# Small matmuls of the delta rule between two feed-forward layers: four groups a chunk instead of six

## The chip, the cores and the metric

The kernel runs on one core of one Trainium2 chip. The metric is the device time in microseconds (us), the median of the runs shown. Lower is better.

## The reference

A delta rule over 768 tokens (4 batches, 8 heads, 48 features a head) feeds two feed-forward layers of 3072 tokens, 384 features and 2048 hidden units:

```python
for t in range(S):
    kt, vt, bt = (k_n[:, :, t], v[:, :, t], beta[:, :, t, None])
    y[:, :, t] = np.einsum('bhd,bhde->bhe', q[:, :, t], state)
    v_old = np.einsum('bhde,bhd->bhe', state, kt)
    state = state + bt[:, :, :, None] * np.einsum('bhd,bhe->bhde', kt, vt - v_old)
# y becomes x: 3072 tokens x 384
h = x @ w_in                      # layer 1
g = np.where(pos, h, np.where(neg, 0.0, (h + beta) ** 2 / (4.0 * beta)))
x = g @ w_out
h = x @ w_in2; r = np.maximum(h, 0.0); out = (r * r) @ w_out2     # layer 2
```

## The kernel before

**The delta rule** goes by 24 chunks of 32 tokens (128 rows: 4 batches x 32 tokens). For each chunk, `chunk_steps` (L391) returns six steps, each a run of 64 small matmuls on TensorE, one for each pair of (head, batch), except the last:

- `ks` (L411): K S, keys times the state, into a bank of PSUM with the tag `att`; VectorE subtracts it from the value (L416).
- `tr` (L418): W R, the inverted triangle times that residual, into another `att` bank; ScalarE copies it to U (L428).
- `qs` (L430): Q S, into an `att` bank that stays in use until `pu` is done. Behind it the keys of the chunk after the next five are loaded on SP (`load_kq(c + 6)`).
- `ku` (L446): K' U, added to the state in its own PSUM banks; VectorE and ScalarE copy the state to SBUF (L456, L457). The last chunk has none.
- `pu` (L437): P U, added to Q S in its bank; ScalarE copies the sum to Y (L444).
- `xt` (L467): three 128x128 transposes of Y, from which ScalarE and VectorE make the input of layer 1 (L476, L477).

The matmuls of `ks` and `qs` have a 48x32 stationary operand, those of `tr` and `pu` one of 32x32, those of `ku` one of 32x48. There are two `att` banks.

**The gram** of a chunk (L260) gives K K' and Q K' by 64 more small matmuls (48x32 stationary) into an `att` bank, which VectorE masks (L284) into `gp`. When four chunks of a group have theirs, `tri` (L314) inverts their triangles: VectorE transposes `gp` (L325), a short run of VectorE, ScalarE and GpSimd instructions scales it, GpSimd does 29 dependent steps of two instructions each (L370, L376), and VectorE transposes the result back (L380). The next group's `tr` needs that.

**Layer 1** goes by nine blocks of 2 or 3 chunks (SIZES) and 16 hidden units of 128 in each. `hidden` makes a unit's nine 128x128 matmuls into the one bank `h` (two sums of hi parts and lo parts: six with `xh`, three with `xl`), ScalarE and VectorE the activation; `out1` takes nine more two units later into the `acc` banks. Layer 2 does the same with eight blocks and no chunk steps beside it.

**The order on TensorE is written out by hand** (`manual_schedule` with PE alone, L660); the order on the other engines is the scheduler's. Each hidden unit of a block has two slots: one right behind `hidden` (L773) and one right behind `out1` (L778), so that a block has 32. The loop at L703 to L719 lists the steps and grams that belong to a block's time (those of the next block's chunks) and spreads them: entry i of n goes to slot i * 32 // n (in the first block over 24 slots, from the ninth on). In a full block that is 18 steps and 3 to 5 grams. `ready` and `at` remember the slots of a gram and of a chunk's first step; `tri` is called one slot after the last gram of its group, its end is called at the slot of the first step that needs it (L733 to L735).

Of the kernel before, what the change touches and what calls it, by code (L numbers as in the profile page):

```python
# [17 lines left out]

# Chunks of the blocks in which the first layer takes them
SIZES = [2, 2, 3, 3, 3, 3, 3, 2, 3]  # L20
# and of the groups whose triangles are inverted together
GROUPS = [4] * 6
# [3 lines left out]
def kernel(  # L26
# [8 lines left out]
):  # L35
    """The delta rule in chunks of T tokens, with keys as they come (K, not normalised):
    with n = |k| + 1e-6 and g = beta / n**2,
        W = inverse(1 + diag(g) strictlower(K K')) diag(g),  U = W (diag(n) V - K S),
        Y = Q S + strictlower(Q K') U,                       S <- S + K' U.
    Its result goes through the two feed-forward layers, whose float32 products are sums of  # L40
    products of exact parts: x = hi + lo, 12 bits each (float32r).

    kq:   [chunk, (batch % 2, feature), (batch // 2, head, key tokens | query tokens)]
    kv:   [chunk, (batch, token), (key | value, head, feature)]
    beta: [(batch, chunk of the group, head), group, token]
    w1, w2: [128 hidden, in | out, partition, column], the bits of float64
    out:  [chunk, (batch, token), feature]
    """
    nc = tc.nc
# [10 lines left out]
    GFIRST = [sum(GROUPS[:g]) for g in range(NG)]  # L60
    GC = T // H               # chunks of a full group
    NM = NCH // NC            # blocks of the second layer
    N = NC * P
    LAG = 2
    LENT = 28                 # weights whose bits may lie in the last weights' place
    RG = 3
    RAW = 3
    WT, WL = 3, 4
    GB = 2
    MANY = 4                  # first hidden units that may use the chunks' banks  # L70
    HEAD = 8                  # slots of the first block without steps of the second's chunks

# [16 lines left out]
    def weight(i, f):  # L89
        """(hi, lo) of hidden units f's weights: in (i = 0), out (1)."""  # L90
        if (i, f) not in pairs:
            t = wp.tile([P, 2, DM], F32R, tag=f"w{i}{f}", name=f"w{i}{f}")
            pairs[i, f] = t[:, 0], t[:, 1]
        return pairs[i, f]

    s_ps = [ps.tile([P, H, D], F32, name=f"sps{i}") for i in range(B2)]

    # Until the first layer begins, its banks serve the chunks too.
    early = ["att", "acc0", "att", "acc1", "acc2"]
# [15 lines left out]

# [1 line left out]
    def load_kq(c, tag="kqt", bufs=6):  # L117
# [13 lines left out]

    # A weight comes as the bits of a float64: words (low, high).  The high word, read as a
    # float32 and scaled by 2**-112, has its exponent rebiased; shifted left by 3 it is the
    # weight's leading 21 bits as a float32.  The low word adds the last 3 bits, rounded to
    # nearest, but never up into the leading ones.
    raws = {}

    # The last weights' place takes some of the first ones' bits.
    def load_w(x, key):
# [6 lines left out]

    # The second layer's weights become float32.
    def convert_stages(key, box):
# [20 lines left out]

    # The first layer's become their two parts, x = hi + lo.  # L170
    def part_stages(key, box):
# [13 lines left out]
    def weight_items(w):  # L185
        # A hidden unit's second weights are needed LAG units after its first.
        keys = [(w, f, i) for f in range(NF) for i in range(2)]
        if w == 0:
            keys.sort(key=lambda k: (k[1] + LAG * k[2], -k[2]))

        def item(x):
            _, f, i = keys[x]
            box = {}
            if w == 0:
                r = part_stages(keys[x], box)
            else:
                r = convert_stages(keys[x], box)
                r.append(lambda: nc.sync.dma_start(w2f[f, :, i], box["t"]))
            s1 = r[1]
            r[1] = lambda: (s1(), ahead(x + 1))  # L200
            return r

        # Loads run ahead of the conversions by the buffers there are.
        todo = list(enumerate(keys))

        def ahead(x):
            end = x + RAW
            if w == 0 and end < LENT:
                end = min(end + 2, LENT)
            while todo and todo[0][0] < end:  # L210
                load_w(*todo.pop(0))

        return lambda: ahead(0), [item(x) for x in range(len(keys))]
# [18 lines left out]

# [1 line left out]
    def norm_stages(ss, sm):  # L234
        """n = sqrt(ss) + 1e-6, the root after one Newton step."""
        return [
            lambda: nc.scalar.activation(sm[0], ss, AF.Sqrt, scale=0.25, bias=tiny),
            lambda: nc.vector.reciprocal(sm[2], sm[0]),
            lambda: nc.vector.scalar_tensor_tensor(
                sm[1], ss, 0.25, sm[2], ALU.mult, ALU.mult),  # L240
            lambda: nc.vector.scalar_tensor_tensor(
                sm[0], sm[0], 1e-6, sm[1], ALU.add, ALU.add),
            lambda: nc.vector.reciprocal(sm[2], sm[0]),
        ]

    def value(c):
        """V becomes diag(n) V."""
        g, j = group_of[c]
        nc.gpsimd.tensor_mul(  # L249
            kvt[c][:, 1], kvt[c][:, 1],  # L250
            nt[g][:, j * H:(j + 1) * H].rearrange("p (h o) -> p h o", o=1)
            .to_broadcast([P, H, D]),
        )
# [6 lines left out]
    def gram(c, lo=0, hi=2, late=0):  # L260
        """K K' (x = 0) and Q K' (x = 1), x from lo to hi; what is returned is left to do
        (if late > 1, to what left its bank)."""
        n, j = group_of[c]
# [30 lines left out]

    # The keys of the first chunks with the keys and queries of those after them, up to the
    # last of the first block: these do without a state.
    HEADS = SIZES[0]
# [11 lines left out]

    # The upper triangle of a chunk's K K', one (batch, chunk, head) a partition; its diagonal  # L310
    # is |k|**2.  x[c, i] becomes W[i, c], each of `parts` (engine, rows) by itself.
    tx = cst.tile([P, T, T], F32, name="tx")
# [74 lines left out]

# [1 line left out]
    us = {}  # L389

    def chunk_steps(c):  # L391
# [4 lines left out]
        def of_state(o, x):  # L396
            """K S (x = 0) or Q S; at first, S is the sum of K' U so far."""
            if c < HEADS:
# [61 lines left out]
        def done():  # L460
            """Of ku and xt, the second makes room."""
            t["n"] = t.get("n", 0) + 1
            if t["n"] == 2:
                del kvt[c]
                load_kv(c + 3)
# [13 lines left out]

        return [ks, tr, qs, pu, ku, xt] if c < HEADS else [ks, tr, qs, ku, pu, xt]  # L480

# [1 line left out]
    x2 = dram.tile([P, KT, NCH * P], F32, name="x2", bufs=1)  # L483
    gs, acc = {}, {}

    def prods(pairs, swap=False):
        """Sums of hi hi + lo hi + hi lo, the right's lo last."""
        def mm(o, l, r, **flags):
# [10 lines left out]
    def hidden(layer, n, f):  # L499
# [12 lines left out]
        if layer == 0:  # L512
            # g = (min(relu(h + 1), 2) / 2)**2 + relu(h - 1)
            marks[0] = nc.scalar.activation(r, h, AF.Relu, bias=one)  # L514
# [68 lines left out]
    def flow(items, lag=1):  # L583
        """The stages of items, each item `lag` steps behind the one before it."""
        steps = []
# [74 lines left out]
    with tc.manual_schedule(engines=ENGINES):  # L660
# [28 lines left out]
        def later(*fs):  # L689
            """These, queued behind what the hidden units need by then."""  # L690
            def one_(f):
# [7 lines left out]

        # The chunks' steps, spread evenly over the slots of the block before theirs; with them  # L700
        # the products of the chunk whose keys take the place of this one's.
        at, ready, due = {}, {}, [GFIRST[2]]
        for n in range(1, NB):  # L703
            todo = []
            for c in range(FIRST[n], FIRST[n] + SIZES[n]):
                left = {0: 1, 1: 1, 2: 0, 3: 2}[c % GC]
                for i, s_ in enumerate(chunk_steps(c)):
                    todo.append(((at, c) if i == 0 else None, s_))
                    x = due[0]
                    if i + left > 5 and x < NCH:  # L710
                        left -= 1
                        due[0] += 1
                        todo.append(((ready, x), lambda x=x: gram(x)))
            for i, (mark, s_) in enumerate(todo):
                o = 0 if n > 1 else HEAD
                slot = SL * (n - 1) + o + i * (SL - o) // len(todo)
                if mark:
                    mark[0][mark[1]] = slot
                put_a(0, slot, s_)  # L719
        for c in range(3, NCH):  # L720
# [113 lines left out]
```

## Time and profile before

| | us |
|---|---|
| median of 3 runs | 1115.31 |
| lowest, highest | 1114.62, 1117.25 |
| span of the profiled execution | 1115.4 |
| TensorE busy (matmul) | 999.2 |
| VectorE busy | 649.7 |
| ScalarE busy | 506.3 |
| GpSimd busy | 315.9 |

In time: the first triangles and chunks to 72 us, the first block of layer 1 to 164 us, the second to 216 us, six more to 653 us, the last of layer 1 to about 705 us, and layer 2 from there to the end. Chunk steps stand beside the blocks from 72 to 653 us. In the rows below a PE row merges neighbouring matmuls of one line and tile, its second column reaches from the first one's start to the last one's end, and the bracket at its end is idle time of the engine ahead of it and what ended that.

### The profile page before, as it was taken

The numbers are of one execution on the slowest core, as the hardware profiler recorded it, in microseconds if no ns is written. First come the engines' busy times: TensorE is split into PE (matmuls) and PEld (weight loads), VectorE is DVE, ScalarE is ACT, GpSimd is POOL, SyncE is SP. The second block draws the span as 40 slices with busy tenths as digits, with TensorE's granted clock in tenths as the row PEclk, the third lists the DMA queues.
The fourth block names the chain that finished last, engine by engine and source line by source line (L and its number), as shares of the span: only waits on it lengthen the run. The fifth ranks groups of instructions, "written<-read, shape, count | busy, mean of one in ns | idle before, by whom it ended". The sixth has DMA issues, their size and how long they took to land.

```text
span 1115.4 us, 32967 instructions
## 1 busy us (share of the span) xinstructions
PE 999.2 (90%) x14312; PEld 955.1 (86%) x14312; DVE 649.7 (58%) x1235; ACT 506.3 (45%) x1068; POOL 315.9 (28%) x462
## 2 busy tenths in 40 slices
PE   4344879979997999699979999899999999999998
PEld 3334879968986999699879999899999999999998
DVE  4999887765684485466654467754344343434333
ACT  1045646635553555365455666433333333333332
POOL 3477760580184029204800021311101010101000
PEclk9966889998998999899989999999999999999999
DMA  8145325133141151141211122201010010000000
GB/s 231 38 143 164 88 87 177 57 100 101 31 151 58 35 165 57 35 152 38 67 36 44 39 87 86 86 1 43 1 43 28 16 43 1 22 1 22 1 22 22
DMA packets 33489, 73.00 MB, mean 65 GB/s; under 512 B 3904, under 2 KB 17728, under 8 KB 33344
## 3 DMA queue, kind: packets, MB, share of 16 engines
q1 hardware_dynamic: 33344, 70.89, 20.9%
q8 instruction: 112, 1.84, 0.7%
q14 instruction: 33, 0.27, 0.1%
HBM read 55.15 MB, written 15.73 MB: 64 GB/s over the span
## 4 chain that ended last, share of the span: by engine, by line
PE 67%; DVE 14%; POOL 11%; issue 5%; ACT 3%; DMA 1%; SPq 0%; DVEq 0%; ACTq 0%; POOLq 0%
PE h L489 30%; PE acc L489 30%; POOL tx L376 5%; POOL t L370 5%; DVE wl L161 2%; DVE wl L158 2%; DVE g L518 2%; DVE wl L164 1%; PE tr L420 1%; PE g L272 1%; DVE tx L376 1%; PE yy L440 1%; DVE t L370 1%; PE yy L406 1%; PE ks L406 1%
## 5 line engine op out<-in xcount | busy, mean ns | idle before, releaser
L489 PE MATMUL h<-xh,w 128*128 128x384 f32 (+1 forms) x1632 | 326.2, 337 | 25.6 <-ACT g L515 25.1
L489 PEld LDWEIGHTS h<-xh,w 128*128 128x128 f32 x1632 | 277.4, 194 | 31.9 <-ACT g L515 25.1
L527 DVE TENSOR_TENSOR gl<-g,gh 128x384 fp32r<-128x384 f32 (+1 forms) x272 | 169.3, 622 | 122.2 <-ACT gh L526 117.0
L526 ACT CAST gh<-g 128x384 fp32r<-128x384 f32 (+1 forms) x272 | 134.5, 494 | 210.7 <-DVE g L518 109.8
L489 PE MATMUL h<-xl,w 128*128 128x384 f32 (+1 forms) x816 | 181.9, 332 | 2.1 <-DVE xl L477 2.1
L489 PE MATMUL acc<-gh,w 128*128 128x384 f32 (+1 forms) x864 | 171.8, 336 | 8.2 <-ACT gh L526 5.6
L521 DVE TENSOR_TENSOR g<-r 128x384 f32<-128x384 f32 x128 | 71.3, 557 | 156.8 <-ACT r L520 156.8
L489 PE MATMUL acc<-w,gh 128*128 128x384 f32 x768 | 155.5, 337 | 1.6 <-DVE e L534 1.6
L489 PEld LDWEIGHTS acc<-gh,w 128*128 128x128 f32 x864 | 140.8, 196 | 13.5 <-ACT gh L526 5.7
L520 ACT ACTIVATE r<-h,zero 128x384 f32<-128x384 f32 x128 | 74.5, 582 | 165.4 <-PE h L489 165.4
L489 PEld LDWEIGHTS h<-xl,w 128*128 128x128 f32 x816 | 143.7, 193 | 2.4 <-DVE xl L477 2.4
L489 PEld LDWEIGHTS acc<-w,gh 128*128 128x128 f32 x768 | 136.3, 188 | 1.9 <-ACT gh L526 1.9
L514 ACT ACTIVATE r<-h,one 128x384 f32<-128x384 f32 (+1 forms) x144 | 78.4, 544 | 84.1 <-PE h L489 82.1
L518 DVE TENSOR_TENSOR g<-g,r 128x384 f32<-128x384 f32 (+1 forms) x144 | 90.3, 627 | 38.3 <-ACT r L517 37.0
L516 DVE TENSOR_SCALAR r<-r 128x384 f32<-128x384 f32 (+1 forms) x144 | 60.5, 420 | 78.4 <-ACT r L514 78.0
L370 POOL TENSOR_TENSOR t<-tx,gm 128x30 f32<-128x30 f32 (+16 forms) x171 | 96.5, 564 | 15.3 <-DVE tx L354 3.5
L376 POOL TENSOR_TENSOR tx<-tx,t 128x30 f32<-128x30 f32 (+16 forms) x171 | 96.7, 565 | 11.9
L489 PE MATMUL acc<-gl,w 128*128 128x384 f32 (+1 forms) x432 | 92.5, 323 | 4.1 <-DVE gl L527 4.1
L249 POOL TENSOR_TENSOR kv<-kv,nt 128x384 f32<-128x384 f32 x24 | 21.5, 901 | 259.9 <-DMA kv<-in_kv_dram 84.6
L517 ACT ACTIVATE r<-r 128x384 f32<-128x384 f32 (+1 forms) x144 | 70.6, 490 | 48.7 <-DVE r L516 47.8
L576 POOL CAST xh<-x2r 128x1152 fp32r<-128x1152 f32 x8 | 9.5, 1187 | 293.1 <-PE h L489 293.1
L489 PE MATMUL acc<-w,gl 128*128 128x384 f32 x384 | 88.0, 337 | 0.0
(85 smaller groups left out, 1032.0 us busy)
## 6 DMA issues: line engine op xcount, KB each, us to landing
raw<-in_w_dram SPq DMA_DIRECT2D x64, 384.0 KB, 3.3
kqt<-in_kq_dram SPq DMA_DIRECT2D x48, 192.0 KB, 4.2
kv<-in_kv_dram SPq DMA_DIRECT2D x24, 384.0 KB, 3.1
w2f<-wl SPq DMA_DIRECT2D x32, 192.0 KB, 2.6
w2r<-w2f SPq DMA_DIRECT2D x16, 384.0 KB, 3.0
x2r<-x SPq DMA_DIRECT2D x8, 576.0 KB, 4.3
out_dram<-e SPq DMA_DIRECT2D x24, 192.0 KB, 1.9
x<-e SPq DMA_DIRECT2D x18, 192.0 KB, 3.6
```

The costliest lines, as they stand in the source:

```text
L158: nc.vector.tensor_scalar(bits, raw[:, :, 0].bitcast(U32), 2.0 ** -29, 7.0, ALU.mult, ALU.min)
L370: eng.tensor_mul(t, x[:, lo:hi, j:j + 1].to_broadcast([P, hi - lo, w]), gm[:, j:j + 1, j + 1:T].to_broadcast([P, hi - lo, w]),)
L376: ins = eng.tensor_add(x[:, lo:hi, j + 1:T], x[:, lo:hi, j + 1:T], t)
L489: nc.tensor.matmul(o, *((r, l) if swap else (l, r)), **flags)
L514: marks[0] = nc.scalar.activation(r, h, AF.Relu, bias=one)
L516: marks[1] = nc.vector.tensor_scalar(r, r, 2.0, 0.5, ALU.min, ALU.mult)
L517: nc.scalar.activation(r, r, AF.Square)
L518: nc.vector.tensor_add(g, g, r)
L520: marks[0] = nc.scalar.activation(r, h, AF.Relu, bias=zero)
L521: marks[1] = nc.vector.tensor_mul(g, r, r)
L526: nc.scalar.copy(ghi, g)
L527: nc.vector.tensor_sub(glo, g, ghi.bitcast(F32))
```

## The change

The steps of a chunk (the third and later ones) come as four entries: `ks` and `qs` one behind the other, `tr`, `ku` and `pu` one behind the other, `xt`. A later chunk's gram no longer is an entry of its own; it goes behind the entry of `ku` and `pu`, and where a chunk has two grams, the second one behind `xt`. A full block of three chunks then has 12 entries on its 32 slots. (The diff also empties comments and docstrings; line numbers stay.)

```diff
-        return [ks, tr, qs, pu, ku, xt] if c < HEADS else [ks, tr, qs, ku, pu, xt]
+        if c < HEADS:
+            return [ks, tr, qs, pu, ku, xt]
+
+        return [lambda: (ks(), qs()), tr, lambda: (ku(), pu()), xt]
...
                 left = {0: 1, 1: 1, 2: 0, 3: 2}[c % GC]
                 for i, s_ in enumerate(chunk_steps(c)):
-                    todo.append(((at, c) if i == 0 else None, s_))
+                    todo.append([((at, c) if i == 0 else None, s_)])
                     x = due[0]
-                    if i + left > 5 and x < NCH:
+                    if i >= 2 and left and x < NCH:
                         left -= 1
                         due[0] += 1
-                        todo.append(((ready, x), lambda x=x: gram(x)))
-            for i, (mark, s_) in enumerate(todo):
+                        todo[-1].append(((ready, x), lambda x=x: gram(x)))
+            for i, fs in enumerate(todo):
                 o = 0 if n > 1 else HEAD
                 slot = SL * (n - 1) + o + i * (SL - o) // len(todo)
-                if mark:
-                    mark[0][mark[1]] = slot
-                put_a(0, slot, s_)
+                for mark, s_ in fs:
+                    if mark:
+                        mark[0][mark[1]] = slot
+                    put_a(0, slot, s_)
```

## Rows read from the trace of the kernel before

**Rows 1.** The page: TensorE's busy share, and its granted clock in 40 slices (tenths)
```profile
PE 999.2 (90%) x14312; PEld 955.1 (86%) x14312; DVE 649.7 (58%) x1235; ACT 506.3 (45%) x1068; POOL 315.9 (28%) x462
...
PEclk9966889998998999899989999999999999999999
```

**Rows 2.** Busy time by stretch: start:end, length, engines, then clock and DMA
```profile
80.00:170.00 90.00, 64.13 (x1368) 59.02 (x1370) 79.48 (x129) 49.59 (x122) 63.27 (x78) 0.79 0.37 111
460.00:530.00 70.00, 70.00 (x1386) 64.45 (x1386) 44.41 (x91) 39.27 (x83) 13.78 (x24) 0.98 0.28 84
```

**Rows 3.** Timeline of PE (start, length, line, matmuls): small groups among wide ones
```profile
304.54 0.68 PE L489 MATMUL h<-xl,w 128*128 128x384 f32 x3
305.06 1.20 PE L489 MATMUL acc<-gh,w 128*128 128x384 f32 x6
306.10 0.69 PE L489 MATMUL acc<-gl,w 128*128 128x384 f32 x3
306.71 0.89 PE L406 MATMUL yy<-st,kqt 48*32 48x48 f32 x64
307.53 1.32 PE L489 MATMUL h<-xh,w 128*128 128x384 f32 x6
308.69 0.68 PE L489 MATMUL h<-xl,w 128*128 128x384 f32 x3
```

**Rows 4.** Groups by line: busy time, mean ns of one small matmul
```profile
L406 PE MATMUL yy<-st,kqt 48*32 48x48 f32 x1408 | 19.5, 204 | 0.0
```

**Rows 5.** Timeline of DVE: the transposes that end a group's triangles
```profile
160.95 2.22 DVE L380 STREAM_TRANSPOSE gp<-tx 128x1024 f32<-128x1024 f32 x1 [0.49 <-POOL tx L376]
...
248.37 2.04 DVE L380 STREAM_TRANSPOSE gp<-tx 128x1024 f32<-128x1024 f32 x1 [7.84 <-POOL tx L376]
...
347.66 2.02 DVE L380 STREAM_TRANSPOSE gp<-tx 128x1024 f32<-128x1024 f32 x1 [8.99 <-POOL tx L376]
...
454.20 2.06 DVE L380 STREAM_TRANSPOSE gp<-tx 128x1024 f32<-128x1024 f32 x1 [11.65 <-POOL tx L376]
...
558.33 2.06 DVE L380 STREAM_TRANSPOSE gp<-tx 128x1024 f32<-128x1024 f32 x1 [5.83 <-POOL tx L376]
```

**Rows 6.** Timeline of PE: its first group after each of the last four
```profile
251.91 2.29 PE L489 MATMUL h<-xh,w 128*128 128x384 f32 x6 [7.96 <-ACT g L515]
...
350.81 1.93 PE L272 MATMUL g<-kqt 48*32 48x64 f32 x64 [7.08 <-DVE gp L284]
...
457.33 1.93 PE L272 MATMUL g<-kqt 48*32 48x64 f32 x64 [9.37 <-DVE gp L284]
...
563.36 2.29 PE L489 MATMUL h<-xh,w 128*128 128x384 f32 x6 [5.95 <-ACT g L515]
```

**Rows 7.** Timeline of PE: the last grams of the four groups
```profile
197.80 1.10 PE L272 MATMUL g<-kqt 48*32 48x64 f32 x64
...
295.63 1.10 PE L272 MATMUL g<-kqt 48*32 48x64 f32 x64
...
401.69 1.10 PE L272 MATMUL g<-kqt 48*32 48x64 f32 x64
...
507.50 1.10 PE L272 MATMUL g<-kqt 48*32 48x64 f32 x64
```

**Rows 8.** Timeline of PE: two of four short waits between a chunk's steps
```profile
316.74 0.55 PE L474 MATMUL xt<-ident,kv 128*128 128x128 f32 x3 [0.61 <-ACT kv L444]
...
323.92 0.88 PE L420 MATMUL tr<-kv,gp 32*32 32x48 f32 x64 [0.93 <-DVE kv L416]
```

**Rows 9.** Timeline of PE: wide groups with no small one between
```profile
586.36 1.20 PE L489 MATMUL acc<-gh,w 128*128 128x384 f32 x6
...
587.92 1.20 PE L489 MATMUL h<-xh,w 128*128 128x384 f32 x6
```

**Rows 10.** Timeline of PE: first wide groups of the eighth and ninth block
```profile
602.81 0.87 PE L489 MATMUL h<-xh,w 128*128 128x256 f32 x6
...
652.99 1.30 PE L489 MATMUL h<-xh,w 128*128 128x384 f32 x6
```

## The prediction

> **What bounds the kernel now.** The page comes first: TensorE is busy 90% of the span, and its granted clock is full in most slices, with single slices at 8 or 9 tenths in the middle [rows 1]. The busy time by stretch says where TensorE sets the pace. In a stretch of layer 1 such as 460 to 530 us it is busy for all of the 70 us; in the first block, 80 to 170 us, only for 64.1 of 90, while VectorE has 79.5 [rows 2]. So a matmul saved is time saved from about 161 us to 653 us, where chunk steps stand beside wide matmuls, and hardly before that: until 160.9 us GpSimd is also at the second group's triangles, for whose end VectorE waits a further 0.49 us [rows 5].
>
> The timeline of VectorE then shows what breaks this rule. Four times it waits for GpSimd at the transpose that ends a group's triangles (L380), for 7.84, 8.99, 11.65 and 5.83 us [rows 5]. The timeline of TensorE has a stop beside each: 7.96, 7.08, 9.37 and 5.95 us, 30.4 us in all [rows 6]. I call these the four holds. Behind each the clock is at its lower level for a while: six wide matmuls take 2.29 us there [rows 6] and 1.32 us elsewhere [rows 3].
>
> **The price of a group of its own.** Nine wide matmuls with nothing small beside them take 1.56 us from start to start (587.92 - 586.36) [rows 9]. One small group in between costs three things [rows 3]: the three matmuls ahead of it take 0.61 us (306.71 - 306.10) instead of 0.52 (305.06 - 304.54), so 0.09; the six behind it take 1.16 (308.69 - 307.53) instead of 1.04 (306.10 - 305.06), so 0.12; and it holds the array for 0.82 (307.53 - 306.71). As a mere stream it would hold it for less: 0.89 us is from the first start to the last end, and one small matmul lasts 0.204 us by its group's mean [rows 4], so 63 steps take 0.69 us and 64 take 0.70. That leaves 0.12 at the exit. The whole edge is 0.09 + 0.12 + 0.12 = 0.33 us a group.
>
> **The change, part by part.** No matmul, copy or DMA is added or taken out; groups lose their edges, and entries move to other slots. I count only what lies behind the first block.
>
> *K S with Q S*: chunks 4 to 23, 20 merges. Both have the same stationary shape and the same state as moving operand, so the second continues the stream. 20 x 0.33 = 6.6 us.
>
> *K'U with P U*: chunks 4 to 22, 19 merges (the last has no K'U). *A gram behind them*: 11 of the grams 9 to 23 (9, 13, 17 and 21 go behind the transposes, which leaves them both edges). Here the stationary shape changes inside the run, from 32x48 to 32x32 to 48x32. No row shows two small groups of different shape side by side at full clock. What it may cost lies between 0 (a stream) and 0.33 (a full edge). I take 0.12, the exit of a small group, since the other 0.21 is lost by the wide matmuls, and none stand there. 30 x (0.33 - 0.12) = 6.3 us; with the ends of the bound, 9.9 or 0.
>
> The Trainium skill (TensorEngine Tiling (Array Packing), Tiling Modes, Key Properties) says that changing the tiling mode, not just the tile, drains TensorE. By it those 30 merges keep a drain each and the sum is the one above; without it 3.6 us more would come off. No row here can show which.
>
> *Spacing.* A full block had some 21 to 23 entries on 32 slots and now has 12: a step comes 2.67 slots behind the one before, not 1.4 to 1.5. The short waits for a step's own copies, 0.93 and 0.61 us [rows 8] and two of 0.3 near 166 and 185 us, should go: 2.1 us. What is late next is the wide group itself. Four of 16 hidden units in a block now have no small group between their first matmul and the next unit's, so ScalarE has just 1.56 us to empty the one bank `h`. The seventh block already has 12 entries for its 32 slots, and there a unit follows without a gap [rows 9]. But it has no grams, and in the others VectorE also has the triangles' preparation. I put 1.5 us for such gaps, from 0 to 4.
>
> *DMA and waits.* The load of a chunk's successor's keys moves three slots ahead with Q S, the load of values stays behind the transposes; both queue on SP with room to spare. K S and Q S together want both `att` banks at once. The bank of Q S was last used by the transposes or by a gram, three to five slots earlier, and is empty by then. W R's bank is freed by the very subtraction that it needs anyway. The state's copies (L456, L457) start no later than before, and the next K S comes two entries, some five slots, behind. I put nothing for all that; if a bank were late, the wide group behind the pair would wait, and with it ScalarE.
>
> **The four holds.** From a group's last gram [rows 7] to VectorE's stop is 42.7, 43.0, 40.9 and 44.9 us (248.37 - 7.84 - 197.80 and so on [rows 5, 7]), however many slots that is: by the lists about 22, 18, 18 and 21, and it ends between half a slot and seven slots ahead of the slot where the end is called. So the place of L380 in VectorE's order goes with the time since the gram, not with the slot of its call. GpSimd's own chain needs 50 to 53 us from the gram. Merging moves the last gram about four slots forward and the hold with it; it stays. From the last gram to TensorE's restart [rows 6, 7] is 54.1, 55.2, 55.6 and 55.9 us, 221 of the 492 us that count. In there GpSimd's chain sets the end. A merge counts only if TensorE's order gets further ahead of L380 by as much; if L380 keeps its place in the order of work, TensorE stops earlier and waits longer. I take half: 12.9 x 221 / 492 / 2 = 2.9 us lost, from 0 to 5.8.
>
> **Sum.** 6.6 + 6.3 = 12.9 of edges, less 2.9 in the windows of the holds, plus 2.1 of short waits, less 1.5 of new gaps: 10.6 us. The profiled execution's span is 1115.4 us and the median 1115.3, so both give 1105 us.
>
> **The rivals.** *Little is left (1111 us).* Every change of shape costs a full edge and the windows swallow all they can: 6.6 x 271 / 492 = 3.6, plus 2.1, less 1.5, is 4.2 us. For it: the chain through GpSimd holds 221 us of the time. Against it: the order on TensorE is written by hand, so the edges surely go. Chance 0.20.
>
> *A bank is late (1115 us).* With Q S right behind K S, TensorE needs the second `att` bank sooner, and the wait takes back what the edge gave: 0.5 us at each of the 20 pairs gives 1115. For it: the grams at two holds waited for such a bank [rows 6]. Against it: outside the holds no group did in the rows. Chance 0.10.
>
> *The holds reach TensorE sooner, slower (1121 us).* Between VectorE's stop and TensorE's, TensorE ran on for 3.4, 5.1, 5.4 and 4.9 us (251.91 - 7.96 - 240.53 and so on [rows 5, 6]), 18.8 in all, on small groups that needed nothing of VectorE. Now such groups stand closer together and the gaps between them are longer. If at each hold TensorE stops at the next wide group, after 1.6 us or less, some 12 us are lost, and up to 18.8 - 2.4 if the stop comes at once: 1105 + 16 = 1121. It is slower than before from a loss of 12.8 us on. For it: W R waits for the subtraction, which may stand behind L380. Against it: on average the same work lies on each slot. Chance 0.11.
>
> *The holds vanish (1071 us).* If L380's place goes by its call after all, four slots of lead (some 9 us) cover waits of 6 to 12 us; 30.4 of stops and about 1 us each at the lower clock (2.29 - 1.32) go: 1105 - 34 = 1071. Against it: the constant 41 to 45 us. Chance 0.07.
>
> **How the numbers follow.** The forecast has 0.52 and by its bounds (edges 6.6 to 16.5, windows, gaps) reaches from 1099 to 1111. The time is 1105 us. For 8 in 10 I take in the second case and the late bank, and below some of the holds' waits: 1097 to 1116; outside stay the vanished holds (0.07) and the slower case (0.11). A measurement of this kernel can tell about 0.2%, 2.2 us, from no change: faster 0.52 + 0.20 + 0.07 = 0.79, the same 0.10, slower 0.11.
>
> **What would show it.** Stretches of 64 matmuls of K S and 64 of Q S without a wide group between, some 1.6 us long. The eighth block has no hold and three chunks without grams: from 602.81 to 652.99 it takes 50.2 us [rows 10], and should lose 3 x 0.33 + 2 x 0.21 = 1.4. Two shapes side by side show their switch directly. Four waits of VectorE at L380, 6 to 12 us each, some 41 to 45 us behind the last gram less what the edges gave. The prediction is wrong if their stops on TensorE sum to under 20 or over 42 us, or if wide groups wait for ScalarE for more than 4 us outside them.

## The result, and the profile after

The changed kernel takes **1122.45 us** (median; 1121.50 to 1123.97) against 1115.81 us of the kernel before on the same chip: a ratio of 1.006, with a 95% interval of 1.0046 to 1.0074. It is slower by 6.6 us; 1105 us was predicted, in a range from 1097 to 1116. The profiled execution of the changed kernel has a span of 1120.1 us, 4.7 more than that of before. The page's first line of busy times, to be read against [rows 1], has TensorE busy for 4.4 us less:

```profile
PE 994.8 (89%) x14312; PEld 956.6 (85%) x14312; DVE 652.8 (58%) x1235; ACT 505.5 (45%) x1068; POOL 317.2 (28%) x462
```

**Where the time went.** The timeline of TensorE gives the first wide group of a block; first two rows of before, then four of after, the beginnings of the second, eighth and ninth block and of layer 2.

```profile
162.74 0.87 PE L489 MATMUL h<-xh,w 128*128 128x256 f32 x6
...
703.85 1.28 PE L489 MATMUL h<-xh,w 128*128 128x384 f32 x6 [1.68 <-ACT g L515]
```

```profile
165.65 0.98 PE L492 MATMUL h<-xh,w 128*128 128x256 f32 x6
...
607.35 0.87 PE L492 MATMUL h<-xh,w 128*128 128x256 f32 x6
...
656.75 1.31 PE L492 MATMUL h<-xh,w 128*128 128x384 f32 x6
...
708.76 1.29 PE L492 MATMUL h<-xh,w 128*128 128x384 f32 x6 [1.70 <-ACT g L518]
```

The first block ends 2.9 us later (165.65 - 162.74). From there to layer 2 the time is 541.1 us before and 543.1 after: 2.0 more, where 10.6 fewer were forecast. Behind that nothing changes.

**What TensorE waited for in those 541 and 543 us** stands in the waits by line (line and tile that waited, what released it, us in all, times, longest); first before, then after.

```profile
PE g L272 <- DVE gp L284: 16.4, 2, 9.4
PE h L489 <- ACT g L515: 14.5, 3, 8.0
PE acc L489 <- DVE e L534: 2.6, 2, 1.6
PE tr L420 <- DVE kv L416: 1.5, 3, 0.9
PE xt L474 <- ACT kv L444: 0.6, 1, 0.6
```

```profile
PE h L492 <- ACT g L518: 16.2, 10, 6.7
PE acc L492 <- DVE e L537: 13.7, 3, 10.9
PE g L272 <- issue: 6.4, 5, 2.3
PE acc L492 <- DVE gl L530: 5.3, 1, 5.3
PE g L272 <- DVE gp L284: 1.9, 1, 1.9
PE acc L492 <- ACT g L518: 0.8, 1, 0.8
PE yy L406 <- DVE xl L477: 0.7, 2, 0.5
```

The sums are 35.6 and 45.0 us, 9.4 more. As the stretch is only 2.0 us longer, 7.4 us less were spent outside these waits: that is what the merging left of its gain. The short waits for a step's own copies (`tr`, `xt`: 2.1 us) are gone, as forecast. Two kinds are new. Five times a gram stops in its middle with nothing to wait for ("issue", 6.4 us). And wide groups find the bank `h` still being read by ScalarE ten times instead of three.

**The four holds** are still there. VectorE's transposes at L380 answer to [rows 5], TensorE's stops to [rows 6] (there are two at the second hold).

```profile
247.67 1.99 DVE L380 STREAM_TRANSPOSE gp<-tx 128x1024 f32<-128x1024 f32 x1 [5.95 <-POOL tx L376]
342.19 2.00 DVE L380 STREAM_TRANSPOSE gp<-tx 128x1024 f32<-128x1024 f32 x1 [6.47 <-POOL tx L376]
450.88 2.01 DVE L380 STREAM_TRANSPOSE gp<-tx 128x1024 f32<-128x1024 f32 x1 [8.98 <-POOL tx L376]
552.65 2.02 DVE L380 STREAM_TRANSPOSE gp<-tx 128x1024 f32<-128x1024 f32 x1 [12.30 <-POOL tx L376]
```

```profile
250.26 1.10 PE L272 MATMUL g<-kqt 48*32 48x64 f32 x64 [1.88 <-DVE gp L284]
...
344.66 1.33 PE L492 MATMUL acc<-gl,w 128*128 128x384 f32 x3 [5.27 <-DVE gl L530]
348.01 2.29 PE L492 MATMUL h<-xh,w 128*128 128x384 f32 x6 [2.02 <-ACT g L518]
...
455.83 2.29 PE L492 MATMUL h<-xh,w 128*128 128x384 f32 x6 [6.66 <-ACT g L518]
...
555.67 2.29 PE L492 MATMUL acc<-gh,w 128*128 128x384 f32 x6 [10.94 <-DVE e L537]
```

The stops are 26.8 us in all, against 30.4 [rows 6]. So 8.7 of the 16.2 us at `h` belong to holds (2.02 + 6.66), and 7.5 do not; before these were 0.6 (14.5 - 7.96 - 5.95).

**The edges** can be read from merged groups in the timeline of TensorE.

```profile
278.11 0.89 PE L406 MATMUL ks<-st,kqt 48*32 48x48 f32 x64
278.81 0.86 PE L406 MATMUL yy<-st,kqt 48*32 48x48 f32 x64
279.60 1.32 PE L492 MATMUL h<-xh,w 128*128 128x384 f32 x6
...
318.40 0.93 PE L451 MATMUL sps<-kv 32*48 32x48 f32 x64
319.27 0.88 PE L440 MATMUL yy<-kv,gp 32*32 32x48 f32 x64
320.08 1.14 PE L492 MATMUL h<-xh,w 128*128 128x384 f32 x5
```

K S takes 0.70 us up to Q S (278.81 - 278.11), the mere stream. K'U takes 0.87 up to P U (319.27 - 318.40): a change of shape costs up to 0.17 more (K'U's own row is 0.04 longer than that of K S, 0.93 against 0.89). P U takes 0.81 up to a gram (195.92 - 195.11 below), 0.11 more. A pair of one shape holds the array for 1.49 us and a pair of two shapes for 1.68, where two groups alone held it for 1.64 (twice the 0.82 of [rows 3]). So the second pair saves nothing in the array itself, only what its wide neighbours lose at a group.

**The stops inside grams** are in the same view. All five stand in runs of three small groups (K'U, P U, gram); one run with the gram's first part, and the other four stops:

```profile
195.11 0.88 PE L440 MATMUL yy<-kv,gp 32*32 32x48 f32 x64
195.92 0.74 PE L272 MATMUL g<-kqt 48*32 48x64 f32 x34
198.94 0.64 PE L272 MATMUL g<-kqt 48*32 48x64 f32 x30 [2.28 <-issue]
...
178.12 0.99 PE L272 MATMUL g<-kqt 48*32 48x64 f32 x56 [1.16 <-issue]
242.42 0.75 PE L272 MATMUL g<-kqt 48*32 48x64 f32 x35 [1.47 <-issue]
291.94 0.76 PE L272 MATMUL g<-kqt 48*32 48x64 f32 x40 [1.10 <-issue]
399.53 1.08 PE L272 MATMUL g<-kqt 48*32 48x64 f32 x60 [0.38 <-issue]
```

No semaphore ends them. The list of DMA queues on the page, and the same list for the window 195.75 to 196.00 us, show what runs beside them (packets, MB, share of the 16 engines' time):

```profile
q8 instruction: 112, 1.84, 0.7%
...
q8 instruction: 1, 0.02, 43.7%
```

TensorE has 14312 matmuls in every kernel here, each with a weight load, and this queue makes 112 loads of 16 KB (1.84 MB / 112): one load for 128 matmuls with their weight loads, 256 instructions. The load that begins at 195.85 us takes 1.75 us (43.7% of 16 engines over 0.25 us). TensorE stops at 196.66 and goes on at 198.94. In each of the five cases a load begins 2.2 to 3.1 us ahead of the restart. The last section shows by a count of the matmuls that the stops stand where a load's instructions begin.

**Why `h` is late** shows at the beginning of the fourth block: a row each of TensorE, ScalarE and VectorE.

```profile
303.55 0.95 PE L492 MATMUL h<-xh,w 128*128 128x384 f32 x2 [2.51 <-ACT g L518]
```

```profile
300.85 0.52 ACT L520 ACTIVATE r<-r 128x384 f32<-128x384 f32 x1 [3.39 <-DVE r L519]
```

```profile
300.04 0.78 DVE L519 TENSOR_SCALAR r<-r 128x384 f32<-128x384 f32 x1
```

ScalarE waited 3.39 us for VectorE's activation step (L519). That stood behind the preparation of a group's triangles (L325 to L354, 293.5 to 300.1 us), so ScalarE came late to the next unit's bank. That unit has no small group in front of it behind which TensorE could wait unharmed. This is the longest of the eight waits outside the holds; the other seven (0.4 to 1.3 us) were not followed.

### The profile page after: what moved, and what is told of

Its sections match the earlier page's. It is cut to its first block, busy times and chain, and to the rows that moved or that the text cites. A ratio compares the mean times of both kernels' runs of the same rounds, so it can differ in the third digit from the quotient of the medians.

```text
span 1120.1 us, 32985 instructions
## 1 busy us (share of the span) xinstructions
PE 994.8 (89%) x14312; PEld 956.6 (85%) x14312; DVE 652.8 (58%) x1235; ACT 505.5 (45%) x1068; POOL 317.2 (28%) x462
## 3 DMA queue, kind: packets, MB, share of 16 engines
q8 instruction: 112, 1.84, 0.7%
## 4 chain that ended last, share of the span: by engine, by line
PE 60%; POOL 15%; DVE 14%; issue 6%; ACT 3%; DMA 1%; SPq 0%; DVEq 0%; ACTq 0%; POOLq 0%
PE acc L492 27%; PE h L492 27%; POOL tx L376 7%; POOL t L370 7%; DVE g L521 2%; DVE wl L158 2%; DVE wl L161 1%; DVE wl L164 1%; PE g L272 1%; DVE t L370 1%; DVE tx L376 1%; PE sps L451 1%; PE yy L440 1%; ACT r L517 1%; DVE gm L325 1%
## 5 line engine op out<-in xcount | busy, mean ns | idle before, releaser
L492 PE MATMUL acc<-gh,w 128*128 128x384 f32 (+1 forms) x864 | 169.5, 333 | 19.5 <-DVE e L537 13.7
L492 PEld LDWEIGHTS acc<-gh,w 128*128 128x128 f32 x864 | 140.7, 195 | 24.6 <-DVE e L537 14.5
L519 DVE TENSOR_SCALAR r<-r 128x384 f32<-128x384 f32 (+1 forms) x144 | 68.0, 472 | 63.1 <-ACT r L517 62.4
L492 PEld LDWEIGHTS acc<-gl,w 128*128 128x128 f32 x432 | 73.9, 194 | 9.6 <-DVE gl L530 9.4
```

The lines of the kernel that those rows point to most:

```text
L492: nc.tensor.matmul(o, *((r, l) if swap else (l, r)), **flags)
L519: marks[1] = nc.vector.tensor_scalar(r, r, 2.0, 0.5, ALU.min, ALU.mult)
```

## The experiments

**Two theories.** *A*: the merging saves its edges, and new costs of its own take them back: stops in runs of three groups, wide groups that wait for `h`, a slower first block. *B*: the four holds decide. L380 stands so early in VectorE's order that what TensorE saves turns into a longer wait there.

**Parts of the change, with L380 left where the scheduler puts it.** First the grams get entries of their own again:

```diff
-                    if i >= 2 and left and x < NCH:
+                    if i + left > 3 and x < NCH:
...
-                        todo[-1].append(((ready, x), lambda x=x: gram(x)))
+                        todo.append([((ready, x), lambda x=x: gram(x))])
```

> The changed kernel with the grams as entries of their own again (K S with Q S and K'U with P U stay together), so 15 to 17 entries on a block's 32 slots. Theory A (what the merging gave was taken back by waits inside runs of three small groups, five of them and 6.4 us in all, and by wide groups that wait for the one bank h behind hidden units with no small group, some 10 us): no wait inside a gram, late first matmuls of h under 4 us in all, 11 edges of 0.21 us come back: 1122.5 - 6.4 - 7 + 2.3 = about 1111 us. Theory B (the holds at the end of a group's triangles set the time, wherever the small groups stand): within 3 us of the changed kernel, 1120 to 1125.

Measured: 1121.68 us (1120.64 to 1122.24), ratio 1.0046 (1.0031 to 1.0061). There is no wait for "issue" left in layer 1 behind the first block, so A's stops do go with the runs of three. But the time hardly moves, as B had it: TensorE's stops at the four holds are 38.3 us here instead of 26.8, and the first block is 2.7 us longer (its end at 168.37 us against 165.65).

Then the grams stay in others' entries, behind the transposes where that is possible (only the first line of the diff above):

> The changed kernel, its 12 entries a block kept, but a chunk's only gram stands behind the transposes instead of behind K'U and P U; of a chunk's two grams the first stays behind K'U and P U. Theory A: waits inside grams remain only in the runs of three that are left (three of them behind the first block), under 2 us instead of 6.4; the waits for the bank h stay, since the entries do: 1122.5 - 4.5 + 8 x 0.21 = about 1120 us. If the waits inside grams have another cause than the length of the run, they stay at 5 or so and the time at 1122 to 1126. Theory B: within 3 us of the changed kernel.

Measured: 1122.14 us, ratio 1.0054 (1.0037 to 1.0070). One "issue" wait is left, of 1.2 us, and the holds stop TensorE for 32.9 us. B's time held again.

Last, only K S and Q S are merged:

```diff
-        return [lambda: (ks(), qs()), tr, lambda: (ku(), pu()), xt]
+        return [lambda: (ks(), qs()), tr, ku, pu, xt]
```

(and the grams in entries of their own, `i + left > 4`).

> Only K S and Q S together; K'U, P U and the grams are entries of their own as before (18 to 20 entries a full block). Theory A: no wait inside a gram, few late first matmuls of h, 20 edges of 0.33 us: 1115.8 - 6.6 = about 1109 us. Theory B: the gain falls into the holds: 1113 to 1119.

Measured: 1126.42 us, ratio 1.0091 (1.0076 to 1.0106): the smallest change is the slowest kernel of all, slower than either theory had it (1109, and 1113 to 1119). VectorE's waits at L380 from 160 to 700 us, in the view of waits, for the kernel before, the changed one, the first and the third experiment:

```profile
DVE gp L380 <- POOL tx L376: 34.8, 5, 11.7
```

```profile
DVE gp L380 <- POOL tx L376: 36.8, 5, 12.3
```

```profile
DVE gp L380 <- POOL tx L376: 41.3, 4, 12.4
```

```profile
DVE gp L380 <- POOL tx L376: 43.9, 5, 11.6
```

Three of these sums take in a wait at the second group's L380, in the first block: 0.49, 3.08 and 1.31 us (in the first experiment it lies ahead of 160 us). At the four holds alone VectorE waits 34.3, 33.7, 41.3 and 42.6 us. Where merging saves TensorE time and no new stop takes it back, VectorE waits longer at L380. That is B's mark. Between the second and the third of these kernels 6.4 us of stops went away, and 0.8 us of time.

**The holds taken away.** `later` is the kernel's own helper that queues work behind the last hidden unit's activation steps on ScalarE and VectorE. Here it takes the end of the triangles (L380):

```diff
-            put(0, z, end)
+            put(0, z, *later(end))
```

In the changed kernel, and then in the kernel before:

> The changed kernel with VectorE's transpose at the end of a group's triangles (L380) queued behind what the hidden unit of its slot needs of VectorE, instead of where the scheduler puts it. If its early place in VectorE's order makes the holds (26.8 us of stops on TensorE), VectorE's four waits there shrink to under 2 us each and the time falls by 20 to 30: 1093 to 1102. If the holds come from the next W R, which needs the result, the stops move there and the time stays at 1118 to 1124.

> The kernel before, with L380 queued behind what the hidden unit of its slot needs, as in the changed kernel with late ends (1087.9 us). Its place was where the scheduler put it in all kernels so far, so this pair shows what the merging is worth with the holds gone. Theory A (merging saves 12.6 us of edges and gives 5 back in waits inside grams, 8 or so at the bank h and 3 in the first block): nothing is left, 1081 to 1090. Theory B (merging is a gain that the holds alone hid): 1097 to 1102, since 1115.8 less 30 of holds and 4 of slow clock is 1082 only if no part of a hold is left, and with the grams four slots later some of it is.

Measured: 1087.86 us (ratio 0.9748, 0.9734 to 0.9763) and 1089.43 us (0.9758, 0.9744 to 0.9773). With L380 late the holds are gone from the changed kernel: VectorE's wait there is zero at all four. In the kernel before, three remain in part: VectorE waits 5.2, 0.9 and 2.1 us, and TensorE's W R, which needs the subtraction (L416) that stands behind L380, stops for 6.3, 0.9 and 3.1 us beside them. So putting L380 late is worth 27 to 35 us. With it the whole change no longer costs 6.6 us; the 1.6 us by which it is ahead are not clear of noise (the intervals overlap), and the 10.3 us of holds that the kernel before still has are more than that.

The same edit on the first and the third experiment:

> The kernel with grams as own entries (1121.7) with late ends. Its holds were 38 us of stops. Theory A: without them its edges are a gain, as no wait inside a gram and few at the bank h stand against them: 1121.7 - 38 - 4 = about 1080, some 7 below the changed kernel with late ends. Theory B: like that kernel, 1085 to 1090.

> The kernel that puts only K S and Q S together (1126.4) with late ends. Its holds were 43.5 us of stops: 1126.4 - 43.5 - 4 = about 1079 by theory A, 5 to 7 us below the kernel before with late ends (20 edges of 0.33). If these kernels differ for another reason than the holds, it stays above the changed kernel with late ends (1087.9).

Measured: 1082.14 us (0.9692, 0.9669 to 0.9715) and 1084.52 us (0.9717, 0.9699 to 0.9734). With L380 late the order turns round: K S with Q S alone is now better than nothing merged, though 5.5 us short of what A had for it, and K'U with P U better still. Only the gram behind them is bad: 1087.86 with it, 1082.14 without.

**The second group's end too.** In the first block the changed kernel has VectorE waiting 3.1 us at the second group's L380 (0.49 before [rows 5]). The sixth experiment with that end late as well:

```diff
-        end1()
...
+        put(0, at[GFIRST[1]], *later(end1))
```

> As the kernel with own grams and late ends, and the second group's L380, which all kernels so far place freely in the first block, queued behind the slot of the first K S that belongs to it. If VectorE's wait there (1.7 to 3.1 us) is what makes the first block longer than before by 3 to 5.6 us, 2 to 4 us come off; if the first block is longer for the order of its other work, nothing changes (within 1.5 us).

Measured: 1077.59 us (1076.62 to 1078.56), ratio 0.9653 (0.9638 to 0.9668). It is the fastest kernel of the study, 39 us under the kernel before measured beside it (1116.84). Its second block begins at 162.8 us, where that of the sixth experiment begins at 169.4.

The same edit on the kernel before, on the changed kernel and on the one with K S and Q S alone, so that four kernels differ in their sources in the merging only:

> The kernel before, with the second group's end (L380 and what follows) queued late too, as the other four are in the run that gave 1089.4 us. Theory A (the first block is late in the changed kernels because VectorE stands longer at the second group's L380): in the kernel before it stands there for 0.49 us only, so there is next to nothing to win: 1087 to 1090 us, layer 1's second block beginning at 161 to 163 us. Rival (whatever is queued late helps, since it puts VectorE's other work ahead of it): 2 to 5 us less, 1084 to 1087 us.

> The changed kernel with all five ends queued late; with four it took 1087.9 us and its second block began at 166.5 us. Theory A (the second group's L380 holds VectorE in the first block): the block begins at 162 to 163 us, so 1083 to 1085 us, about 4 us under the kernel before with the same late ends. Rival (the first block is late because its small groups are crowded into fewer, larger entries): it stays at 166 us and the time at 1087 to 1088 us.

> Only K S with Q S merged, all ends late; with four late ends it took 1084.5 us with the second block at 162.4 us, and the kernel with K'U and P U merged too and all ends late took 1077.6 us. Theory A (each merge is worth its edges where no hold stands): the first block has nothing to win, so 1083 to 1085 us; the 19 merges of K'U with P U are then worth 6 to 7 us, of which the edges are 19 x 0.21 = 4. Rival (the 1077.6 us came from the late end of the second group alone): 1077 to 1079 us.

| all ends late | us (lowest to highest) | ratio to before (95%) |
|---|---|---|
| nothing merged | 1088.98 (1088.00 to 1092.79) | 0.9766 (0.9743 to 0.9789) |
| K S with Q S | 1085.19 (1084.28 to 1086.15) | 0.9724 (0.9705 to 0.9743) |
| and K'U with P U | 1077.59 (1076.62 to 1078.56) | 0.9653 (0.9638 to 0.9668) |
| and the gram behind them | 1086.69 (1085.77 to 1088.21) | 0.9740 (0.9723 to 0.9757) |

A's time held for the kernel before (its second block begins at 160.8 us) and for K S with Q S alone; it failed for the changed kernel, whose second block begins at 164.7 us and not at 162 to 163. Of its 2.9 us in the first block the second group's L380 explains 1.0 (165.65 - 164.67). For the kernel before the rival of that run is out: a late end where VectorE hardly waited brings nothing (1088.98 against 1089.43). The two pairs of merges bring 3.8 and 7.6 us, 11.4 together, and the gram takes 9.1 back; the ends of the first step's intervals meet, the other two are clear.

These steps are not edges alone. Behind the first block, by the profiled executions, the time outside TensorE's listed waits falls by 3.5 us with K S and Q S and by 3.1 with K'U and P U, where the prediction had 6.6 and 4.0 (19 x 0.21), and by 0.3 with the gram, where it had 2.3 (11 x 0.21). The rest is waits. Parts of holds are among them: W R, or the bank that it waits for, still stops TensorE beside an L380 for 10.3, 7.6, 6.7 and 0 us in the four kernels, in the order of the table.

**The bank `h`.** The changed kernel with all ends late gets a second bank for 16 of the 32 first products that have no small group ahead of them (`half` holds the chunks whose Q S is still in its bank):

```diff
+        x = NF * n + f
+        alone = layer == 0 and 0 < n < NB - 1 and not {2 * x - 2, 2 * x - 1} & taken
-        bank = "att" if many and f % 3 else "h"
+        bank = "att" if many and f % 3 or alone and not half else "h"
```

> The changed kernel with all ends late, and 16 of the 32 first products that have no small group ahead of them (those at which no Q S result is being kept) go to a small group's bank instead of the one bank of h. Theory A (these products wait for ScalarE to clear the bank): among those are the two that began 2.7 and 1.2 us late in the changed kernel with four late ends, so 3 to 4 us less than the changed kernel with all ends late, about 1080 to 1081 us. Rival (the same lateness of ScalarE and VectorE meets the next product, of acc, which needs gh and gl): the wait moves there, and the time stays within 1 us of the kernel without the second bank.

Measured: 1092.83 us (1091.92 to 1093.58), ratio 0.9794 (0.9777 to 0.9810): 6.1 us slower than without it. Neither theory had that. The two products meant (1.0 and 1.2 us late without the second bank) begin on time, but all waits at `h` fall only from 8.4 to 7.4 us, and a new one appears:

```profile
PE yy L406 <- ACT g L523: 3.3, 8, 0.5
```

It is Q S (and, for 1.3 us more, K S and a gram) that now finds ScalarE reading `h` in one of the two banks that the merged pair wants at once. The wait was handed on, and the bank cost more than it gave.

**What is bad in the gram.** All ends late, as many entries as in the change, but no run of three groups: a gram goes behind the transposes or, as the first of two, behind W R.

```diff
-                    if i >= 2 and left and x < NCH:
+                    if left and i in (1, 3) and i + left > 2 and x < NCH:
```

> All ends late; a gram stands behind the transposes, or, as the first of two, behind W R, so that there are as few entries as in the full change (1086.7 us) but no run of more than 256 small matmuls. Theory A (the stops inside runs of three make the difference): no waits for issue inside the grams, so 5 to 6 us less than the full change, 1080 to 1081 us. Rival (it is the units with no small group, which are as many here): the waits for ScalarE at h stay at 8 us and the time at 1085 to 1087 us.

(The 256 are instructions: the 128 matmuls of two groups with a weight load each.) Measured: 1082.02 us (1080.96 to 1082.79), ratio 0.9688 (0.9673 to 0.9702), 4.7 us less than the 1086.69 of the full change. TensorE's waits in layer 1, first of the full change with all ends late, then of this one:

```profile
PE h L492 <- ACT g L518: 8.4, 10, 2.0
PE g L272 <- issue: 5.8, 5, 1.7
```

```profile
PE g L272 <- ACT kv L428: 7.3, 3, 4.0
```

The stops are gone, as A had it, and some of the waits at `h` too (8.4 to 5.7 us); the gain is 1 us short of A's 5 to 6. What is new is a gram behind W R that waits for ScalarE to empty the bank (7.3 us), more than the 4.4 us by which this kernel lies above 1077.6.

The opposite: runs of three in another place. In the kernel of 1077.6 us the last gram of a chunk goes behind the next chunk's K S and Q S.

```diff
+                    if i == 0 and carry:
+                        todo[-1].append(carry.pop())
...
-                        todo.append([((ready, x), lambda x=x: gram(x))])
+                        e_ = ((ready, x), lambda x=x: gram(x))
+                        if left:
+                            todo.append([e_])
+                        else:
+                            carry.append(e_)
```

> The kernel of 1077.6 us (all ends late, grams in entries of their own), but the last gram of a chunk goes behind the next chunk's K S with Q S, which makes runs of three groups in another place. Theory A (TensorE runs out of instructions in a run of three, wherever it stands): stops inside those grams of 0.4 to 2.3 us, 5 of them in about 10 runs, 5 to 6 us, so 1081 to 1084 us. Rival (the stops belong to the place behind K'U and P U, or to chance): no stop inside a gram, 1075 to 1078 us, the edges of some 10 entries being saved.

Measured: 1113.47 us (1107.79 to 1115.76), ratio 0.9964 (0.9950 to 0.9979), far above both. The waits in layer 1:

```profile
PE g L272 <- DVE kv L416: 18.4, 7, 6.6
...
PE g L272 <- issue: 4.3, 3, 1.6
```

A's stops come in this place as well (4.3 us inside grams, and 0.6 each in a Q S and in a wide group). But the largest loss is something that neither had: K S and Q S hold both `att` banks, and the gram right behind them must wait until VectorE has subtracted K S. That subtraction (L416) stands behind L380 in VectorE's order where a chunk is the first of its group, and 15.7 of the 18.4 us lie there. At one of these places the subtraction begins at 260.23 us:

```profile
258.28 2.03 DVE L380 STREAM_TRANSPOSE gp<-tx 128x1024 f32<-128x1024 f32 x1 [2.55 <-POOL tx L376]
```

```profile
260.78 1.93 PE L272 MATMUL g<-kqt 48*32 48x64 f32 x64 [6.56 <-DVE kv L416]
```

So this kernel brought a part of the holds back, at the gram.

## Why the prediction was wrong

**What held.** The edges as sizes: K S runs into Q S as one stream (0.70 us); two shapes side by side cost 0.11 and 0.17 us, where 0.12 was taken between 0 and 0.33. By the Trainium skill (TensorEngine Tiling (Array Packing), Tiling Modes, Key Properties) a change of mode drains TensorE; the trace agrees, with those 0.11 and 0.17 us. The short waits went (2.1 us). The holds stayed, with waits of 6 to 12 us at L380, and stopped TensorE for 26.8 us, inside the bounds of 20 and 42 that were set for them.

**The check block was half right.** The eighth block takes 49.40 us (656.75 - 607.35) instead of 50.2 [rows 10]: 0.8 less, not 1.4. With K S and Q S alone merged it takes 49.09, 1.1 less, or 0.36 for each of three pairs. The two pairs of K'U and P U give nothing there: with them the block is 0.3 us longer. That block's wide matmuls have 256 columns, and I had taken the price of the neighbours (0.21) from 384; that this is the reason was not tested.

**The step that failed first: "I put nothing for all that", under DMA and waits.** I looked for banks and loads of data and not at TensorE's own instructions. Runs of three groups are 192 matmuls in some 2.4 us, and a load brings 128: 6.4 us of stops, in a term that stood at zero. That stops of this size need runs of three is shown by these kernels: they are in the changed kernel with free and with late ends (6.4 and 5.8 us), come back in another place (4.3 us), and with grams in entries of their own or behind W R no gram stops; what is left in shorter runs is 0.2 to 0.3 us a stop, four in all. That they stand where a load's instructions begin is shown by the count in the last section; that the load comes too late for them is argued from its time.

**The second: "I put 1.5 us for such gaps, from 0 to 4".** It was 7.5 us at `h`, 6.9 more than before; "more than 4 us outside the holds" was named as a sign of a wrong forecast, and it came. The mechanism was seen, its size was taken from the seventh block, which has no grams. A unit without a small group leaves no slack when VectorE comes late with the activation, as the fourth block shows; for the shorter waits that is argued. The second bank did not show that this wait can be had back: it moved.

**The third: nothing was put for the first block.** It loses 2.9 us, of which the second group's L380 explains 1.0. With the second group's end late it still begins its successor at 164.7 us, against 162 to 163 in the kernels without the gram behind K'U and P U. Why that gram costs some 2 us in there stays open.

**Summed** by the profiled executions: 7.4 us gained outside the listed waits, 3.6 at the holds, 2.1 of short waits; lost 6.9 at `h`, 6.4 in grams, 1.7 in smaller waits and 2.9 in the first block. That is 4.8 slower, as the spans are. Of the 12.9 us of edges some 5 are not in the 7.4; some 2.5 of them are lateness that the list of waits leaves out (by the starts of the matmuls, those over 0.3 us later than the median of their kind, told by the matmul and the one ahead of it, sum to 11.9 us more than before, not 9.4), the rest was not traced. The bounds of the forecast also reach further than the 1099 to 1111 that it gives for them: taken to their ends they run from 1097 (16.5 + 2.1 = 18.6 us won) to 1114 (6.6 x 271 / 492 + 2.1 - 4 = 1.7 us won), and the result lies outside these too.

**The holds: "I take half: 2.9 us lost, from 0 to 5.8".** In the changed kernel they did not grow but shrank by 3.6 us; my reading is that TensorE lost the time elsewhere first. Where it did not, they did grow, so the term was right in kind and too small: 32.9 us of stops with one stop inside a gram, 38.3 with none, about 43.5 with K S and Q S alone. So with L380 in its place even a merge without the stops and without units that lost their group came out slower: K S and Q S alone take 1126.4 us, and 1085.2 against 1089.0 with all ends late. The first rival's full edge at a change of shape did not come (0.17 us, not 0.33). The second rival, a late bank, cost 0.7 us (`yy` behind `xl`). The third came nearest in time (1121 us), but not in its mechanism, for in the changed kernel the holds cost TensorE less than before. The rival of vanished holds gave 1071 us for the change; the holds are worth what it said (1122.4 - 1086.7 = 35.8 us for 34), but only L380 queued late removes them. Its place does not go by the time since the gram alone: VectorE's stop comes 45.8 us (247.67 - 5.95 - 195.92) behind the last gram at the first hold, 45.4 and 43.1 at the next two and 37.4 at the last, and with the end late it does not come at all in the changed kernel.

## What to carry to other kernels

Before pricing edges on the busiest engine, look for the waiting instruction that stands in front of other work in another engine's in-order queue, and move it behind that work first: here that gave 27 us without any merging, and with it the two pairs of merges turned from 5.9 us lost to 11.4 us won. Merge small groups that share a shape and a moving operand; let a run end before a whole load's instructions lie inside it (here 128 matmuls), and before it needs one bank more than it holds. A unit that loses its small group also loses the slack in which another engine could be late.

## What the runs showed of the hardware

TensorE's stops inside runs of small groups stand where a load of its instructions begins. The view of busy time by stretch counts the matmuls from the beginning of the span; here up to the first and up to the last of the changed kernel's five stops (start:end, length, TensorE's busy time and its matmuls, then clock and DMA):

```profile
0.00:177.50 177.50, 104.26 (x2776) 0.85 0.42 126
...
0.00:399.30 399.30, 303.58 (x7119) 0.91 0.35 106
```

The five come after 2776, 3288, 4182, 5204 and 7119 matmuls. Divided by 128 these leave 88, 88, 86, 84 and 79. With all ends late the same five come at the same counts, 0.7 to 15 us earlier. The stops of the other kernels fit in: after 4182 with grams behind the transposes, after 3416, 4948, 6864, 8780 and 9291 with grams behind K S and Q S (88, 84, 80, 76, 75), and those of 0.2 to 0.3 us in shorter runs, after 3160, 8398, 5460 and 10442 (88, 78, 84, 74). So the place in the program decides: one point in every 128 matmuls. It moves slowly with the count; why was not followed.

Why only long runs stop there is worked out from the same records. In the changed kernel the 128 matmuls ahead of each stop take 1.7 to 1.8 us, all of them small, and a load begins 2.2 to 3.1 us ahead of the restart: TensorE runs through one load's instructions in less time than the next load takes to be of use. Wide matmuls last longer (128 of them some 22 us, by 9 in 1.56 us [rows 9]), and in layer 2, which has no others, no such stop is seen. Why a load does not begin earlier is not shown.

By the Trainium skill (Runtime: NRT & Kernel Launch, Instruction fetch mechanics) instructions come in blocks of 16 KiB, 256 of them, and a crossing is mostly hidden. The block's size agrees with the trace (112 loads for 14312 matmuls and as many weight loads). The hiding held but for 0.2 to 0.3 us in runs of one and two small groups, and not in runs of three, where a stop cost 0.2 to 2.3 us.
